# Two gated-convolution and feed-forward layers on one core: when plane loads are queued, how many dummies stand at the beginning, and in which order transposes run

## The chip, the core and the metric

The kernel runs on one core of a Trainium2 chip. The core has five engines with queues of their own: PE (matmuls; PEld is its weight load), DVE, ACT and POOL (vector, activation and general work) and SP, which here only issues DMAs. POOL issues DMAs too, between its small operations. The metric is the device time of one execution in microseconds (us).

## What is computed

Two layers, each a gated long convolution (A) and a feed-forward block (B), on 2048 tokens of 576 features, in bfloat16. The inner width of B is 4608. Cut to what matters:

```python
def A(q, k, v):
    k_shift = sum(k_pad[:, t:t + S, :] * shift_k[:, 3 - t] for t in range(4))
    kv = k_shift * v
    y = irfft(rfft(kv, 2 * S) * rfft(ssm_k, 2 * S))[:S] + kv * ssm_D
    return q * y

def B(x):
    return (gelu(x @ w_gate) * (x @ w_up)) @ w_down

x = x + A(layernorm(x), A_k, A_v);  x = x + B(layernorm(x))
x = x + A(layernorm(x), A_k, A_v);  x = x + B(layernorm(x))
```

## The kernel before

**Tiling.** The tokens are cut into four chunks of 512 (`CH`). One layer of one chunk is a unit; eight units run in five passes. A pass goes three times through a third of the inner width (12 tiles of 128, `FP`): first `gu`, the gate and up products (L1010: for each tile 18 matmuls of 64 rows and 512 columns, gate and up side by side in the two halves of the array, 1.94 us a tile), then `dn`, the product with `w_down` (L1603, 96 matmuls of 288 columns). All units read all weights again. `load_wgu` (L778) brings four tiles' weights in three DMAs of SP's queue (576, 512 and 64 KB) into one of three buffers, `load_wd` (L788) half a third of `w_down`.

**The convolution.** It is computed once for both layers, chunk by chunk (m = 0 to 3), as block products in the frequency domain. The filter's block transforms lie in DRAM as planes `Hd[b][t]`, those of kv as `Kd[b][t]`. `Conv.step(m)` puts the work of a chunk into lists: `L` (loads), `V` (DVE: kv, then products `prod` at L316 to L320 of a kv plane and a filter plane) and `Pq` (PE: forward transforms L301, inverse L343). For a product of an earlier chunk's kv, `load(kt, a)` issues two DMAs on POOL's queue: a kv plane into `kr` (L418, three buffers) and a filter plane into `hr` (L422, four buffers), 288 KB each; for a product of its own kv only the second. The products of chunk m read the transforms `kc` of that chunk as well, marked in `at` under `("kc", kt, s, h)` when their making is planned.

**What sets the order.** The whole program is written out in advance. `Pace` keeps a planned time for PE (`t.pe`), DVE and ACT. Between matmuls `fill` (L1069) calls `weights()` (issues what `when_due` has put down and that is due), `conv.run_loads()` (pops `L` while its first entry's ready time is reached; before that `flush` writes out what is due of `spills`, a list of POOL work: stores and the small operations `nm`, `ve` and `rstd` of the layer norms), and then DVE, ACT and PE work as far as the planned times allow. The order in which these calls come is the order on each engine's queue. On the chip only semaphores count: an instruction waits for its operands and buffers, and everything behind it on its queue waits with it. `hurry()` is true while the second chunk's convolution isn't finished.

**Layer norm.** For each 128 tokens: `x_c` (DVE L894) is made by the gate, `nm` (POOL L842) is the mean, `junk` (ACT L850) sums squares, `ve` and `rstd` (POOL L857, L858) follow, then `xn` (DVE L923) and its transposition `xnT` by two DMA transposes of SP's queue (L965), which the next unit's `gu` reads.

**The beginning.** Up to about 47 us the order comes from `Plan.order`, a list scheduler with durations and priorities. 20 dummy matmuls (L1141) run first; then come the taps (L1199, which spread the shift weights over the partitions) with two dummies (`spare`, L1192), the sum of the shifted products (L1228), transposes of the filter (L1257 for the first 512 positions, L1277 for the next), the forward transforms (L281, L275), the inverse (L1363), dummies in `busy` (L1382) and the transposes of the first `xn` (L1467, L1469). D = 576 is four times 128 and a rest of 64, so a transposition over D has blocks of 128 and of 64 rows; `turn_xn` has eight full blocks and, for b = 4, two halves of 64 columns.

Of the kernel before, what the change touches and what calls it, by code (L numbers as in the profile page):

```python
# [17 lines left out]
P = 128  # L18
# [8 lines left out]
NEVER = 1e9  # L27
# [10 lines left out]
LAG = 0.25  # L38
AHEAD = 2.0
SLOW, PRESS = 6.0, 22.0  # L40
HOLD, SOON, LEAD, FAR = 14.0, 30.0, 1.8, 3.6


class Pace:
# [88 lines left out]
class Conv:  # L133
# [9 lines left out]
    def __init__(self, tc, ctx, pace, A_k, A_v, A_shift_k, A_ssm_k, A_ssm_D, ident, cps, ypool):  # L143
        self.tc, self.nc, self.t = tc, tc.nc, pace
        self.k2, self.v2, self.hk = A_k[0], A_v[0], A_ssm_k
        self.S, self.D = self.k2.shape
        self.NB = self.S // BS
        self.KS = A_shift_k.shape[1]
        self.sk, self.sD = A_shift_k, A_ssm_D
        self.ident, self.cps, self.ypool = ident, cps, ypool  # L150
        D = self.D
        pool = lambda name, bufs: ctx.enter_context(tc.tile_pool(name=name, bufs=bufs))
        self.cst = pool("c_cst", 1)
        self.krp = pool("c_kr", 3)
        self.hrp = pool("c_hr", 4)
        self.kcp = pool("c_kc", N_KC)
        self.ybp = pool("c_yb", 4 * RT)
        self.prp = pool("c_pr", 3)
        self.acp = pool("c_ac", 3)
        self.eop = pool("c_eo", 2)  # L160
        self.kvp = pool("c_kv", 1)
        self.Hd = [[tc.dram_tile([P, 2 * D], BF16, name=f"Hd{b}_{t}") for t in range(RT)] for b in range(self.NB)]
        self.Kd = [[tc.dram_tile([P, 2 * D], BF16, name=f"Kd{b}_{t}") for t in range(RT)] for b in range(self.NB - 1)]
        self.hs = {b: tc.dram_tile([BS, D], BF16, name=f"hs{b}") for b in range(2, self.NB)}
        self.T = self.cst.tile([P, RT, 2, P], BF16, name="T")
        self.nT = self.cst.tile([P, 5, P], BF16, name="nT")
        self.V_ = self.cst.tile([P, 2, RT, P], BF16, name="V")
        self.nV = self.cst.tile([P, 3, P], BF16, name="nV")
        self.skc = self.cst.tile([P, self.KS, D], BF16, name="skc")
        self.y, self.yb, self.hh = {}, {}, {}  # L170
        self.kt_, self.vt_ = {}, {}
        self.y_at = {(0, j): 0.0 for j in range(RT)}
        self.z_at = {0: 0.0}
        self.kv_at, self.fwd_at, self.hf_at, self.hd_at = {}, {}, {}, {}
        self.ht = {}
        self.y_used = {}
        self.ps_free, self.cur, self.alt, self.alt_at = [0.0, 0.0], 0, None, None
        self.neo, self.eo_at = 0, deque([0.0] * 2)
        self.U = deque()
        self.kr_free, self.hr_free = [0.0] * 3, [0.0] * 4  # L180
        self.nkr = self.nhr = 0
        self.V, self.L, self.Pq = deque(), deque(), deque()
        self.left = 0
        self.spills = deque()
# [184 lines left out]
    def step(self, m, kv=None, loaded=False):  # L369

        nc, D, t = self.nc, self.D, self.t
        kc, kr, hr, z, nyb, prs = {}, {}, {}, {}, {}, {}
        KTS = (0, 2, 1, 3)
        at = {}
# [48 lines left out]
                at[("ld", kt, a)] = t.pe + 8.0  # L423
            return run
        for kt, a in pairs:
            self.L.append((lambda a=a: max(self.hr_free[self.nhr % 4], self.hd_at.get(m, NEVER) if a == 0 else 0.0,
                                           self.kr_free[self.nkr % 3] if a < m else 0.0),
                           load(kt, a)))

# [100 lines left out]
        w = {}  # L530
# [165 lines left out]
def ssm_geglu_kernel(ctx, tc, A_q, A_k, A_v, A_shift_k, A_ssm_k, A_ssm_D, B_x, B_w_gate, B_w_up,  # L696
# [4 lines left out]
    S, D = q2.shape  # L701
# [9 lines left out]
    NKC = D // HK  # L711
# [8 lines left out]
    t = Pace()  # L720
# [33 lines left out]
    def pr(name):  # L754
        while late and taken[0] - late[0][1] >= 2:
# [15 lines left out]
    conv = Conv(tc, ctx, t, A_k, A_v, A_shift_k, A_ssm_k, A_ssm_D, ident,  # L771
                lambda *form: bank(turn[3], "cps", *form), ypool)
# [274 lines left out]
    def weights():  # L1047

        while due:
            near = xn_made or (vq and isinstance(vq[0][0], tuple) and vq[0][0][0] == "xn")  # L1050
            if due[0][0] > t.pe + (HOLD if near else SOON):
                break
            _, _, load, n = due.pop(0)
            load(n)

    coming, due_at = [0], [0.0]

# [33 lines left out]
    with tc.manual_schedule():  # L1091
# [3 lines left out]
        ND = D // P + 1  # L1095
        plan = Plan(4)
        add = plan.add
        with ExitStack() as es:
# [38 lines left out]
            warm = tmp.tile([P, 1], F32, name="warm")  # L1137
            nc.scalar.activation(out=warm[:], in_=conv.pis[:], func=ACT.Sin)
            ps = bank(3, "ps")
            for _ in range(20):  # L1140
                nc.tensor.matmul(ps[:, 0, 0:P], lhsT=ones[:], rhs=ones[:], start=True, stop=True)  # L1141

            held = {}
# [44 lines left out]
            vneg = add("ACT", 0.9, vnegs, [vsin], prio=-20.0)  # L1188

            def spare(ps):  # L1190
                for _ in range(2):
                    nc.tensor.matmul(ps[:, 1, 3 * P:4 * P], lhsT=ones[:], rhs=ones[:], start=True, stop=True)  # L1192


# [15 lines left out]
            for i0 in range(0, RT, 2):  # L1210
                accs = {i0: [], i0 + 1: []}
                first = {}
                for j in range(conv.KS - 1, -1, -1):
# [9 lines left out]
                    for i in (i0, i0 + 1):  # L1223
# [7 lines left out]
                        a = later(lambda me: add("PE", 0.25, me(acc), [mults[-1]], bank=(j == conv.KS - 1), prio=20.0))  # L1231
# [16 lines left out]
            def turned_h0():  # L1248
                outs = []
                hT[0] = lambda i: hT0[:, i, :]  # L1250
                for g in range(RT // 2):
                    def fill_ps(task, g=g):
                        pt = psum(("h", g), task, (P, 2, 1024), BF16)
                        for i in range(2):
                            for db in range(ND):
                                w = min(P, D - db * P)
                                nc.tensor.transpose(pt[:, i, db * P:db * P + w], hn[0][0:w, db, 2 * g + i:BS:RT], ident[0:w, 0:w])  # L1257
                    a = later(lambda me: add("PE", 1.05, me(fill_ps), bank=True, ready=HN_AT, prio=30.0))
                    outs.append(add("ACT", 1.12, lambda g=g: nc.scalar.copy(out=hT0[:, 2 * g:2 * g + 2, :], in_=held.pop(("h", g))[:, :, 0:D]),
                                    [a], lat=0.1, frees=[a], prio=30.0))  # L1260
                return outs

            def turned_h1(dep):


                W = D - P
                beside = lambda j: held["y", j].bitcast(BF16)
                hT[1] = conv.ht[1] = lambda i: pairs1[i // 2][:, i % 2, :]
                for g, j in ((0, 3), (1, 1)):
                    def fill_ps(g=g, j=j):  # L1270
                        pairs1.append(conv.hrp.tile([P, 2, D], BF16, tag="hr", name="ht"))
                        for i in range(2):
                            for db in range(ND):
                                w = min(P, D - db * P)
                                out = beside(j)[:, i, 2 * HW + (db - 1) * P:2 * HW + (db - 1) * P + w] if db else \
                                    beside(0)[:, g, 2 * HW + i * P:2 * HW + (i + 1) * P]
                                nc.tensor.transpose(out, hn[1][0:w, db, 2 * g + i:BS:RT], ident[0:w, 0:w])  # L1277
                    a = add("PE", 1.0, fill_ps, dep + [opened[0], opened[j], facs[j]], prio=-30.0)
                    add("DVE", 0.2, lambda g=g: nc.vector.tensor_copy(
                        out=pairs1[g][:, :, 0:P], in_=beside(0)[:, g, 2 * HW:2 * HW + 2 * P].rearrange("p (i d) -> p i d", i=2)),  # L1280
                        [a], frees=[opened[0]], prio=-10.0)
                    add("ACT", 0.84, lambda g=g, j=j: nc.scalar.copy(
                        out=pairs1[g][:, :, P:D], in_=beside(j)[:, :, 2 * HW:2 * HW + W]), [a], lat=0.1, frees=[opened[j]], prio=-20.0 if g else -30.0)
# [25 lines left out]
            kc, A = {}, {}  # L1309
            K0 = {}  # L1310
            for m in KTS:
                K0[m] = []
                for s in range(2):
                    def fill_ps(task, m=m, s=s):
                        if s == 0:
# [3 lines left out]
                    a = later(lambda me: add("PE", 0.99, me(fill_ps), list(kv0.values()) + [tneg if m else tsin], bank=True,  # L1319
                                           prio=-4.0 * KTS.index(m)))  # L1320
# [85 lines left out]
            for j in (0, 2, 1, 3):  # L1406
# [52 lines left out]
                def turn_xn(task, j=j):  # L1459
                    if 0 not in xnT_of:  # L1460
                        xnT_of[0] = xtp.tile([P, NKC, CH], BF16, tag="xnT", name="xnT")
                    pt = psum(("xt", j), task, (P, 2, 1024), BF16)
                    for b in range(NKC):
                        c0 = b * P if b < 5 else HK + (b - 5) * P
                        if b == 4:
                            for r0, c0 in ((0, 4 * P), (HK, 0)):
                                nc.tensor.transpose(pt[r0:r0 + HK, 0, 4 * P:5 * P], held["xn", j][:, c0:c0 + HK], ident[:])  # L1467
                            continue
                        nc.tensor.transpose(pt[:, b // 8, (b % 8) * P:(b % 8 + 1) * P], held["xn", j][:, c0:c0 + P], ident[:])  # L1469
# [49 lines left out]
        hurry = lambda: (1, RT - 1) not in conv.y_at  # L1519
# [4 lines left out]
        for at, (wb, ph, ui, first, final) in enumerate(visits):  # L1524
# [33 lines left out]
            for fi in range(FP):  # L1558
                n, gi = divmod(wb * FP + fi, FG)
                w = wgu[n]  # L1560
# [141 lines left out]
```

## Time and profile before

| | |
|---|---|
| median of 3 runs (lowest, highest) | 926.32 us (924.35, 926.99) |
| the profiled execution | 929.08 us |
| its span, from the first to the last instruction | 927.3 us |
| PE busy | 917.8 us |
| gu (L1010), busy; dn (L1603), busy | 563.6 us; 294.1 us |
| granted clock of PE, mean | 0.996 |
| DMA moved | 129.69 MB |

The profile's page gives busy times by engine, the chain of work that ended last, and groups of instructions. Other views of the same trace are the timeline (start, length, engine, line, operation, tiles, count, and in brackets the idle time before it and what ended it), the list of waits (in total, times, longest) and windows (busy time of each engine in a stretch). A matmul's length includes its way through the array; the distance of two starts is what it costs in a row. The clock column counts only what the profiler recorded.

### The profile page before, as it was taken

The page shows a single profiled execution, that of the slowest core. Times are in us where ns is not written, and L with a number is a line of the kernel's source. Part 1 is how long each engine was busy: PE and PEld are TensorE (multiplying, and loading weights), DVE is VectorE, ACT ScalarE, POOL GpSimd, SP SyncE. Part 2 cuts the span into 40 slices and gives each one's busy share as a digit, 9 for nine tenths or more (in the row PEclk, how much of TensorE's full clock was granted, in tenths as well). Part 3 has the DMA queues.
Part 4 walks back from the last instruction along what each step waited for, and adds up shares of the span by engine and source line. Part 5 has one row for each costly group of instructions (what it writes and reads, how often), then busy time and mean ns, then how long its engine had stood idle before and what let it go on. Part 6 is the DMA issues. An engine that isn't in the chain of part 4 may idle for free.

```text
span 927.3 us, 19211 instructions
## 1 busy us (share of the span) xinstructions
PE 917.8 (99%) x8085; PEld 526.5 (57%) x8085; DVE 558.8 (60%) x1106; ACT 364.7 (39%) x675; POOL 141.2 (15%) x314
## 2 busy tenths in 40 slices
PE   9999999999999999989999999999999999999998
PEld 6746556465565564636646646546556556556555
DVE  7885887883889886548988943553332334433332
ACT  6774436635425366344253332451221224321211
POOL 4413102320114012410121101220000002100000
PEclk9999999999999999989999999999999999999999
DMA  9999997369518602982953720692820731777640
GB/s 231 274 243 204 265 269 165 91 177 205 179 54 201 165 1 40 271 171 72 244 172 100 136 78 27 125 158 52 153 78 2 144 87 14 132 175 180 125 106 27
DMA packets 125307, 129.69 MB, mean 140 GB/s; under 512 B 39714, under 2 KB 117411, under 8 KB 125220
## 3 DMA queue, kind: packets, MB, share of 16 engines
q1 hardware_dynamic: 116018, 92.92, 47.9%
q0 software_dynamic: 9056, 34.95, 11.7%
q8 instruction: 63, 1.03, 0.5%
q10 hardware_dynamic: 146, 0.59, 0.2%
q14 instruction: 24, 0.20, 0.1%
HBM read 108.09 MB, written 11.80 MB: 129 GB/s over the span
## 4 chain that ended last, share of the span: by engine, by line
PE 94%; DMA 4%; issue 1%; ACT 0%; DVE 0%; POOL 0%; SPq 0%; ACTq 0%; POOLq 0%; DVEq 0%
PE gu L1010 58%; PE dn L1603 30%; DMA wgu<-in_B_w_up_dram 2%; DMA Hd<-hh 2%; PE ps L281 1%; PE cps L343 1%; PE cps L301 1%; PE ps L1228 1%; PE ps L1363 1%; PE ps L1010 0%; PE ps L1257 0%; DMA sk<-in_A_shift_k_dram 0%; PE cps L290 0%; PE ps L275 0%; PE ps L1277 0%
## 5 line engine op out<-in xcount | busy, mean ns | idle before, releaser
L1010 PE MATMUL gu<-xnT,wgu 64*128 64x512 bf16 x5148 | 563.6, 377 | 4.4 <-DMA wgu<-in_B_w_up_dram 4.0
L1010 PEld LDWEIGHTS <-wgu 64*128 64x128 bf16 x5220 | 252.2, 94 | 312.1 <-issue 9.9
L1603 PE MATMUL dn<-wd,hT 128*128 128x288 bf16 x2304 | 294.1, 286 | 0.0
L1603 PEld LDWEIGHTS <-hT 128*128 128x128 bf16 x2304 | 223.6, 98 | 65.0 <-issue 7.2
L1584 ACT ACTIVATE ga<-gu 128x512 f32<-128x512 f32 x175 | 104.5, 597 | 331.2 <-PE gu L1010 328.1
L1585 DVE TENSOR_TENSOR hT<-ga,gu 128x512 bf16<-128x512 f32 x175 | 120.2, 687 | 183.7 <-ACT ga L1584 183.6
L1574 ACT ACTIVATE ga<-gu 128x512 bf16<-128x512 f32 x111 | 66.4, 598 | 156.2 <-PE gu L1010 148.5
L1576 DVE TENSOR_TENSOR hT<-ga 128x512 bf16<-128x512 bf16 x112 | 47.0, 422 | 61.5 <-ACT ga L1575 61.2
L1575 ACT CAST ga<-gu 128x512 bf16<-128x512 f32 x111 | 64.4, 581 | 0.0
L842 POOL TENSOR_SCALAR means<-s 128x1 f32<-128x1 f32 x28 | 9.5, 341 | 245.0 <-DVE x_c L1639 206.9
L1647 DVE TENSOR_TENSOR x_c<-x_c,dn 128x576 f32<-128x576 f32 x32 | 24.1, 752 | 27.4 <-PE dn L1603 27.2
L1645 DVE SCALAR_TENSOR_TENSOR x_c<-dn,means,x_c 128x576 f32<-128x576 f32 x28 | 22.8, 816 | 26.2 <-PE dn L1603 26.2
L858 POOL TENSOR_TENSOR rstd<-ve,neghalf_t 128x1 f32<-128x1 f32 x56 | 34.9, 623 | 4.7
L320 DVE TENSOR_TENSOR prod<-prod 128x576 bf16<-128x576 bf16 x72 | 33.0, 458 | 2.5
L303 ACT ACTIVATE eo<-cps 128x576 f32<-128x576 f32 x32 | 20.5, 654 | 20.9 <-DVE ab L308 9.2
L1626 DVE TENSOR_TENSOR xn<-x_c,dn 128x576 bf16<-128x576 f32 x15 | 11.3, 754 | 27.9 <-PE dn L1603 27.9
L418 POOL DMA_DIRECT2D kr<-Kd x24 | 13.2, 552 | 85.0 <-DVE prod L319 84.6
L604 DVE TENSOR_TENSOR kc<-ab,cd 128x288 bf16<-128x288 f32 x64 | 25.4, 453 | 0.0
L422 POOL DMA_DIRECT2D hr<-Hd x36 | 19.6, 547 | 36.9 <-DVE prod L319 36.6
L842 POOL TENSOR_SCALAR nm<-s 128x1 f32<-128x1 f32 x28 | 8.5, 305 | 94.3 <-DVE x_c L894 94.3
L884 ACT ACTIVATE yh<-y,rstd 128x576 f32<-128x576 bf16 x28 | 21.4, 769 | 2.6 <-POOL rstd L858 2.3
L850 ACT ACTIVATE junk<-x_c,nm 128x576 bf16<-128x576 f32 x28 | 21.5, 767 | 2.0 <-POOL nm L842 1.9
(180 smaller groups left out, 611.6 us busy)
## 6 DMA issues: line engine op xcount, KB each, us to landing
wgu<-in_B_w_gate_dram SPq DMA_DIRECT2D x45, 576.0 KB, 6.3
wd<-in_B_w_down_dram SPq DMA_DIRECT2D x30, 864.0 KB, 7.1
wgu<-in_B_w_up_dram SPq DMA_DIRECT2D x45, 512.0 KB, 8.3
hr<-Hd POOLq DMA_DIRECT2D x36, 288.0 KB, 6.4
kr<-Kd POOLq DMA_DIRECT2D x24, 288.0 KB, 4.3
Kd<-kc POOLq DMA_DIRECT2D x12, 288.0 KB, 5.3
k<-in_A_k_dram POOLq DMA_DIRECT2D x3, 1008.0 KB, 11.2
wgu<-in_B_w_up_dram SPq DMA_DIRECT2D x45, 64.0 KB, 8.5
```

Of the source, the lines that this page charges most:

```text
L320: nc.vector.tensor_tensor(out=dst[:, cols], in0=pr[:, 0, cols], in1=pr[:, 1, cols], op=ALU.subtract if part == 0 else ALU.add)
L604: nc.vector.tensor_tensor(out=into[k][:, plane, cols], in0=a, in1=b, op=op)
L858: nc.gpsimd.tensor_tensor(out=v["rstd"][:], in0=ve[:], in1=neghalf_t[:, 0:1], op=ALU.pow)
L1010: nc.tensor.matmul(cols(pair[:, s, :]), lhsT=w[r0:r0 + HK, k, gi * P:(gi + 1) * P], rhs=cols(xnT[r0:r0 + HK, blk_of[k], :]), start=(k == 0 ...
L1574: nc.scalar.activation(out=ga[:, 0, :], in_=pair[:, 0, :], func=ACT.Gelu_apprx_tanh)
L1575: nc.scalar.copy(out=ga[:, 1, :], in_=pair[:, 1, :])
L1576: nc.vector.tensor_tensor(out=hT[:, fi, :], in0=ga[:, 0, :], in1=ga[:, 1, :], op=ALU.mult)
L1584: nc.scalar.activation(out=ga[:], in_=pair[:, 0, :], func=ACT.Gelu_apprx_tanh)
L1585: nc.vector.tensor_tensor(out=hT[:, fi, :], in0=ga[:], in1=pair[:, 1, :], op=ALU.mult)
L1603: nc.tensor.matmul(acc[:, h, 0:HW], lhsT=hT[:, fi, j * P:(j + 1) * P], rhs=wd[2 * wb + fi // WT][:, fi % WT, h * HW:(h + 1) * HW], start=( ...
L1645: nc.vector.scalar_tensor_tensor(out=xh, in0=acc[:, :, 0:HW], scalar=m_[:, 0:1], in1=xh, op0=op, op1=ALU.add)
L1647: nc.vector.tensor_tensor(out=xh, in0=xh, in1=acc[:, :, 0:HW], op=ALU.add)
```

## The change

Planned loads of planes get one more condition. `weights()` now sets `conv.quiet` to ten planned microseconds after each weight load that it issues, unless `hurry()`; a plane load of `step` isn't popped before `quiet` unless the transform `("kc", 0, 0, 0)` of its chunk is planned already. In the program that results, DVE, ACT and SP have the same instructions in the same order as before. On POOL one place differs: seven plane loads (three `kr`, four `hr`) of chunk 3 stood ahead of three `nm`, one `ve` and one `rstd`, and now stand behind these five.

```
before: out_dram, kr, hr, kr, hr, kr, hr, hr, nm, nm, nm, ve, rstd, ve, rstd, nm, ve, rstd
after:  out_dram, nm, nm, nm, ve, rstd, kr, hr, kr, hr, kr, hr, hr, ve, rstd, nm, ve, rstd
```

The dummies at the beginning are 24, not 20, and those of `spare` 5, not 2. In L1257 and L1277 the loop over the blocks of D goes outside, so that the four blocks of two tiles come in a row: eight transposes of 128 rows and then two of 64, where before it was four, one, four, one. In `turn_xn` block 4 comes last: eight full ones and then the two halves, where before the halves stood between four and four.

```diff
-HOLD, SOON, LEAD, FAR = 14.0, 30.0, 1.8, 3.6
+HOLD, SOON, QUIET, LEAD, FAR = 14.0, 30.0, 10.0, 1.8, 3.6
...
+        self.quiet = 0.0
...
         for kt, a in pairs:
-            self.L.append((lambda a=a: max(self.hr_free[self.nhr % 4], self.hd_at.get(m, NEVER) if a == 0 else 0.0,
+            self.L.append((lambda a=a: max(0.0 if ("kc", 0, 0, 0) in at else self.quiet, self.hr_free[self.nhr % 4], self.hd_at.get(m, NEVER) if a == 0 else 0.0,
                                            self.kr_free[self.nkr % 3] if a < m else 0.0),
                            load(kt, a)))
...
             _, _, load, n = due.pop(0)
             load(n)
+            if not hurry():
+                conv.quiet = t.pe + QUIET
...
-            for _ in range(20):
+            for _ in range(24):
                 nc.tensor.matmul(ps[:, 0, 0:P], lhsT=ones[:], rhs=ones[:], start=True, stop=True)
...
             def spare(ps):
-                for _ in range(2):
+                for _ in range(5):
                     nc.tensor.matmul(ps[:, 1, 3 * P:4 * P], lhsT=ones[:], rhs=ones[:], start=True, stop=True)
...
-                        for i in range(2):
-                            for db in range(ND):
-                                w = min(P, D - db * P)
+                        for db in range(ND):
+                            w = min(P, D - db * P)
+                            for i in range(2):
                                 nc.tensor.transpose(pt[:, i, db * P:db * P + w], hn[0][0:w, db, 2 * g + i:BS:RT], ident[0:w, 0:w])
...
-                    for b in range(NKC):
+                    for b in sorted(range(NKC), key=lambda b: b == 4):
```

The loop at L1272 to L1277 is turned in the same way as that of L1257.

More of the change, by code (lines that the diff above doesn't have):

```diff
@@ L1271, in fill_ps @@
                         pairs1.append(conv.hrp.tile([P, 2, D], BF16, tag="hr", name="ht"))
-                        for i in range(2):
-                            for db in range(ND):
-                                w = min(P, D - db * P)
+                        for db in range(ND):
+                            w = min(P, D - db * P)
+                            for i in range(2):
                                 out = beside(j)[:, i, 2 * HW + (db - 1) * P:2 * HW + (db - 1) * P + w] if db else \
```

## The prediction

> **What bounds the kernel now.** I read the page first, then PE's waits, then the two places that these name.
>
> ```profile
> PE 917.8 (99%) x8085; PEld 526.5 (57%) x8085; DVE 558.8 (60%) x1106; ACT 364.7 (39%) x675; POOL 141.2 (15%) x314
> PE 94%; DMA 4%; issue 1%; ACT 0%; DVE 0%; POOL 0%; SPq 0%; ACTq 0%; POOLq 0%; DVEq 0%
> ...
> PE gu L1010 <- DMA wgu<-in_B_w_up_dram: 4.0, 1, 4.0
> PE gu L1010 <- DMA wgu<-in_B_w_gate_dram: 0.3, 1, 0.3
> ```
>
> PE is busy for 99% of the span, so time can come only from three things: PE work that goes, idle of PE, and PE work done at a lower rate. The list of waits has one idle of size: 4.0 us, once, for a weight load. In time, it stands here: PE's timeline, then windows (length, busy time of PE, PEld, DVE, ACT and POOL, granted clock, DMA share, GB/s).
>
> ```profile
> 383.41 15.71 PE L1010 MATMUL gu<-xnT,wgu 64*128 64x512 bf16 x144
> 399.44 0.39 PE L1010 MATMUL gu<-xnT,wgu 64*128 64x512 bf16 x1 [0.32 <-DMA wgu<-in_B_w_gate_dram]
> 403.88 10.26 PE L1010 MATMUL gu<-xnT,wgu 64*128 64x512 bf16 x71 [4.05 <-DMA wgu<-in_B_w_up_dram]
> ...
> 399.00:401.80 2.80, 0.51 (x3) 0.09 (x1) 2.22 (x7) 0.60 (x1) 0.95 (x3) 1.00 1.16 167
> 401.80:408.60 6.80, 4.72 (x24) 1.73 (x26) 0.00 (x0) 0.61 (x2) 0.00 (x0) 0.50 1.27 202
> 408.60:412.00 3.40, 3.40 (x34) 1.53 (x32) 1.79 (x4) 1.82 (x4) 0.97 (x2) 1.00 0.62 61
> ```
>
> The stall costs more than its idle. 71 matmuls take 10.26 us, where the row before has 144 in 15.71 (0.109 each, 7.75 for 71): the granted clock was 0.50 from 401.8 to 408.6, and PE worked 403.88 to 408.6 at half rate, a loss of 4.72 / 2 = 2.36. The place as a whole costs 0.32 + 4.05 + 2.36 = 6.7 us. What delayed the load is read from SP's timeline, the chain (one line, start and length) and POOL's timeline:
>
> ```profile
> 380.28 0.91 SPq L783 DMA_DIRECT2D wgu<-in_B_w_gate_dram  x1
> 381.24 3.51 SPq L784 DMA_DIRECT2D wgu<-in_B_w_up_dram  x1
> ...
> 381.24 22.59 DMA wgu<-in_B_w_up_dram
> ...
> 385.10 0.55 POOL L418 DMA_DIRECT2D kr<-Kd  x1
> ...
> 394.83 0.19 POOL L857 TENSOR_SCALAR ve<-ss 128x1 f32<-128x1 f32 x1 [1.03 <-ACT junk L850]
> 395.11 0.57 POOL L858 TENSOR_TENSOR rstd<-ve,neghalf_t 128x1 f32<-128x1 f32 x1
> 396.72 0.19 POOL L857 TENSOR_SCALAR ve<-ss 128x1 f32<-128x1 f32 x1 [1.04 <-ACT junk L850]
> ```
>
> The weight load of 1152 KB (576 + 512 + 64) is issued at 380.28 and lands 22.59 us after its second part, where the page's median is 6.3 to 8.5. Between 385.10 and 389.2 POOL issues seven plane loads (three kr, four hr, 288 KB each, 2016 KB); they land 8.6 to 13.2 us after issue, so by 401.9, beside the weights. The second place is the beginning, in PE's timeline:
>
> ```profile
> 1.08 2.31 PE L1141 MATMUL ps<-ones 128*128 128x128 bf16 x20 [1.08 <-DVE ones L1113]
> 3.61 2.20 PE L1199 MATMUL ps<-sk,ones 97*128 97x288 bf16 x8 [0.22 <-DMA sk<-in_A_shift_k_dram]
> 5.63 0.39 PE L1192 MATMUL ps<-ones 128*128 128x128 bf16 x2
> 6.09 1.11 PE L1228 MATMUL ps<-kvt,below 128*128 128x288 bf16 x4
> 7.00 2.96 PE L1257 MATMUL ps<-ident,hn 128*128 128x128 bf16 x20
> 12.71 0.61 PE L1184 MATMUL ps<-ident,T 128*128 128x128 bf16 x8
> ```
>
> Matmuls of 128 columns start every 0.107 us up to here (20 in 2.1) and every 0.056 from 12.71: PE runs at half rate for its first 11.6 us, though the clock column shows 1.00 there (the records begin later). Holes are small: 0.22 at 3.39, 0.06 at 6.03, and in L1257 each change between 128-row and 64-row transposes.
>
> **The change, part by part.** *Plane loads behind weights.* Every queue keeps its order and its waits but POOL's (and PE's, below). There three nm, one ve and one rstd pass ahead of the seven loads. These five are ready no earlier than now (nm at 389.66 to 393.60 after DVE, ve at 394.83 after ACT), so the loads are issued from 395.11 + 0.57 = 395.7 on, 10.6 us later, to about 399.5 (seven of 0.55). Their bytes are gone from the stretch in which the weights come. The windows of 5 us from 386 on show 262 to 308 GB/s; 2.06 MB at 300 is 6.9 us, so the last part lands at about 403.8 - 6.9 = 396.9. A second estimate: two such loads issued at 598.8 and 600.9, without planes, land 7.8 and 11.5 us after issue of their last parts, 5.7 us apart; the load before ours lands at 391.05 now, plus 5.7 is 396.8. PE needs it at 399.1: covered by 2.2 us. Gain 6.7, all there is. The lower bound is 2.4: the two estimates are off by 4 us, 2.0 of the 4.4 us of idle and the half rate stay. A loss here is excluded, since no byte is added ahead of the load.
>
> What is moved and what it now meets: the second ve and rstd, 396.72 to 397.54 now, stand behind the loads and end at about 399.5 + 0.9 = 400.4. Their reader is DVE's second xn (L923), which starts at 400.50 after a product of hT: free, by 0.1 us. Uncovered, each us would push the hT products behind it, of which PE stands one bank (1.94 us) off. The third rstd comes at 401.4, its xn about 6.7 us earlier than 409.23: free by 1. The planes land some 10 us later, by about 411; the first product that reads them (L316) starts at 435.39, 428.7 with the gain: free by 17. The transposes of xnT (L965, first at 399.27) meet the planes where they met weights and planes; their longest now is 8.6 us, the last issue would be at 409.4, the landing by 418, the next gu at 427.9 - 6.7 = 421.2: free by 3.
>
> *Transposes.* L1257 in the cold stretch: a visit to the 64-row form takes 0.244 + 0.170 + 0.089 for three starts, against 0.107 + 0.107 + 0.053 without a change: 0.24 each, four visits become two, 0.47 off PE. L1228 behind it has its operand at 9.10 and starts at 9.89, so that it can follow. If the half rate still ends at 12.7, work that slides in front of it runs cold, and half of the 0.47 remains: 0.25. L1277 (four visits of 0.385 for 0.167): 0.44 off PE at 38.5, but the DVE copy behind it can start only when the xn before it ends (39.43 against 39.55): 0.13. The xn transposes L1467 lose their last change before gu: 0.15 to 0.17 less 0.15 that L1010 then pays: 0. Sum 0.4; bounds 0.1 and 0.9.
>
> *Dummies.* Four more at 0.107 are 0.43 us in the hole before L1199, whose operand comes at 3.48 and which starts at 3.61: the last one starts at 3.50, cost 0 (0.1 at most). Three more behind the first tap: 0.32 us from 5.82, L1228 slides from 6.09 to 6.14: cost 0.05. The ACT copy of that tap waits for them too, 0.3 us, and its product on DVE comes at about 7.1: covered. What they can bring is an earlier full rate. No row shows such a thing with these holes filled, so bounds: 0, and for full rate from 6 us on 2.6. The latter because ACT then binds: its sine ends at 7.75, two copies of 1.12 and the table load of 1.28 follow, so the V copy comes at 11.5, not 13.36, and with 0.74 us of ACT idle at 17.28 that is 1.9 + 0.7. For one step of 3.4 us earlier it is about 1.5. The restart after the stall is the nearest row: full rate came back 4.7 us after matmuls went on without a hole. By it a stretch without holes from 1.08 to 7.5 would be enough. But 97 of 128 rows in L1199 and the transposes may count for less. I take 1.0.
>
> [...]
>
> **Sum.** Against the profiled execution's own 929.08 us (span 927.3 and 1.8 around it): 6.7 + 0.4 + 1.0 = 8.1, 921.0. The median of the runs shown, 926.32, is 2.8 below that execution. Part of this may be a smaller stall, since its half-rate share hangs on when the clock falls: between 0.32 + 4.05 = 4.4 without it and 6.7. I take 6.0 for timed runs: 926.3 - 6.0 - 0.4 - 1.0 = 918.9.
>
> **Rivals.** *A: the weights still come late* (the loads before them, wd behind them and four out stores crowd the queue as well; SP needs 3.51 us to issue one part, before any plane load stands there). For: the load is slow from 380.3 on, planes from 385.1. Against: the 2.2 us of cover. Price: 1 to 2 us of idle and the half rate are left, gain 2.4 to 3.3: 923.5. *B: only the beginning moves or nothing does*, the stall being smaller in runs that aren't profiled. For: the 2.8 us between them. Against: bytes and order are the same. Gain 0 to 1.5: 925.5. *C, slower: the planes now crowd xnT.* All seven start with the transposes at 395.7 to 399.5. If the last xnT comes later than 421.2, PE idles at the next gu and loses clock as at 401.8; with half rate (2.4) it needs 5 us of idle to eat up 7.4, a landing at 426, 17 us after issue. Against: 8.6 is the longest now with more bytes in flight. 928. *D, within the forecast: no earlier full rate:* 919.9; with it 917.5 to 918.4.
>
> **Chances.** Forecast 0.80 (D half of it), A 0.10, B 0.06, C 0.04. Low end: 6.7 + 0.9 + 2.6 = 10.2 below 926.3 is 916.1, less some of the runs' spread (924.35 to 926.99): 915.5. High end 923.5, where A stands. A measurement of this kernel tells 0.3% (2.8 us, 923.5) from no change. Faster: 0.80 + half of A + a little of B, 0.86; same: 0.09; slower: C and strays, 0.05.
>
> **What would show it.** PE's list of waits without L1010 <- wgu; no 0.50 clock near 400; kr and hr issued at 395.7; xn's second L923 still at about 400.5; L1277 shorter by 0.4; the step from 0.107 to 0.056 us per dummy or transpose before 9.3 (or still near 12.7: D). A wait of gu near 421 would be C, one near 399 A.

## The result and the profile after

The changed kernel takes 918.76 us (median of 9 runs, 918.59 to 922.95), the kernel before 925.8 (9 runs, 921.59 to 927.67): ratio 0.9936, 95% interval 0.9917 to 0.9954, so 4.3 to 7.7 us less. The profiled executions differ by more: 929.08 before and 918.68 after, 10.4 us, with spans of 927.3 and 916.9. All but one of the nine runs after lie within 1 us of each other; the one at 922.95 has a granted clock of 0.998 where the others have 0.999 or 1.0.

The page of the changed kernel, busy times and the chain that ended last by engine:

```profile
PE 911.7 (99%) x8092; PEld 524.9 (57%) x8092; DVE 558.5 (61%) x1106; ACT 364.2 (40%) x675; POOL 142.6 (16%) x314
...
PE 99%; POOL 0%; ACT 0%; DVE 0%; issue 0%; ACTq 0%
```

PE's list of waits, whole:

```profile
PE ps L1144 <- DVE ones L1116: 1.1, 1, 1.1
PE ps L1472 <- DVE xn L1458: 0.5, 2, 0.3
```

(Line numbers are one higher from the constructor of the planner on and three higher in the beginning.) The wait for wgu has left the list, and DMA has left the chain. PE's busy time fell by 6.1 us though it runs 7 matmuls more: what fell is in the main the part at half rate, at the beginning and behind the stall. PE's timeline of the pass that held the stall:

```profile
380.30 23.48 PE L1011 MATMUL gu<-xnT,wgu 64*128 64x512 bf16 x216
```

POOL's timeline there:

```profile
391.99 0.57 POOL L859 TENSOR_TENSOR rstd<-ve,neghalf_t 128x1 f32<-128x1 f32 x1
392.52 0.63 POOL L419 DMA_DIRECT2D kr<-Kd  x1
...
396.98 0.56 POOL L859 TENSOR_TENSOR rstd<-ve,neghalf_t 128x1 f32<-128x1 f32 x1
```

And the issue of the last part of the weights, with its time to landing:

```profile
L786 SPq DMA_DIRECT2D wgu<-in_B_w_up_dram x1: 1052/1052/1052, 380.7 to 380.7; - x1
...
DMA to landing us min/median/max: 12.9/12.9/12.9
```

The pass is now 216 matmuls without a break in 23.48 us. Plane loads begin when the first rstd is done; the weights land at 380.7 + 12.9 = 393.6, where PE, 15.7 us into its pass (its matmuls before the stall took 15.71), needs them at 396.0.

The beginning in PE's timeline:

```profile
1.08 2.74 PE L1144 MATMUL ps<-ones 128*128 128x128 bf16 x24 [1.08 <-DVE ones L1116]
3.88 2.20 PE L1202 MATMUL ps<-sk,ones 97*128 97x288 bf16 x8
5.90 0.46 PE L1195 MATMUL ps<-ones 128*128 128x128 bf16 x5
6.36 0.65 PE L1231 MATMUL ps<-kvt,below 128*128 128x288 bf16 x4
6.84 1.62 PE L1260 MATMUL ps<-ident,hn 128*128 128x128 bf16 x20
9.88 0.61 PE L1187 MATMUL ps<-ident,T 128*128 128x128 bf16 x8
```

The half rate ends before 6 us: five dummies of 128 columns now fit into 0.46, four matmuls of 288 columns into 0.65 (1.11 before). The trace's clock record begins at 5.03 us, with full rate; before, at 12.67. From the starts of the same instructions in both timelines the 10.4 us can be laid out:

| start of | before | after | earlier by |
|---|---|---|---|
| the first matmul with weights | 42.88 | 40.11 | 2.77 |
| the second gu pass | 87.67 | 84.55 | 3.12 |
| the gu pass with the stall | 383.41 | 380.30 | 3.11 |
| the next gu pass | 427.90 | 417.54 | 10.36 |

So 2.8 us come from the beginning, 0.35 from the stretch up to the second pass (in the kernel before PE waits there for ACT's `eo`, 0.2 us at 83 us), and 7.25 from the stalled pass.

### The profile page after: what moved, and what is told of

Same layout as the page of the kernel before. It is cut to its first block, busy times and chain, and to the rows that moved or that the text cites. A ratio compares the mean times of both kernels' runs of the same rounds, so it can differ in the third digit from the quotient of the medians.

```text
span 916.9 us, 19225 instructions
## 1 busy us (share of the span) xinstructions
PE 911.7 (99%) x8092; PEld 524.9 (57%) x8092; DVE 558.5 (61%) x1106; ACT 364.2 (40%) x675; POOL 142.6 (16%) x314
## 4 chain that ended last, share of the span: by engine, by line
PE 99%; POOL 0%; ACT 0%; DVE 0%; issue 0%; ACTq 0%
PE gu L1011 61%; PE dn L1606 31%; PE ps L282 1%; PE cps L291 1%; PE cps L344 1%; PE cps L302 1%; PE ps L1231 0%; PE ps L1011 0%; PE ps L1366 0%; POOL rstd L1451 0%; PE ps L1144 0%; PE ps L1202 0%; PE ps L276 0%; PE cps L1027 0%; ACT yh L1413 0%; PE ps L1260 0%
## 5 line engine op out<-in xcount | busy, mean ns | idle before, releaser
L419 POOL DMA_DIRECT2D kr<-Kd x24 | 13.3, 554 | 85.8 <-DVE prod L320 84.1
```

## Experiments

Times are medians, ratios are to the kernel before as it ran beside each set of experiments. Its medians there were 925.8 (with the changed kernel), 926.13 (e1 to e4), 926.38 (e5 to e8) and 927.65 (e9 to e12; 8 runs), so a difference of about 1 us between rows of different sets isn't shown by the times alone. "First gu" is the start of the first matmul with weights, "full rate" the begin of the clock's record, both from the profiled execution; "pass" is the time from the start of the gu pass near 380 us to the start of the next one. A window, in the expectations and below, is a stretch of 3.41 us: the half clock lasted that long in e2's profile (0.50 from 400.0 to 403.4) and twice that, 6.83 us, in the kernel before (401.79 to 408.62).

| label | us (runs) | ratio, interval | first gu | full rate | pass |
|---|---|---|---|---|---|
| before | 926.13 (35) | | 42.88 | 12.67 | 44.49 |
| after | 918.76 (9) | 0.9936, 0.9917 to 0.9954 | 40.11 | 5.03 | 37.24 |
| e1_loads | 921.79 (12) | 0.9951, 0.9931 to 0.9970 | 43.23 | 13.58 | 37.24 |
| e2_begin | 923.17 (12) | 0.9967, 0.9946 to 0.9987 | 40.04 | 4.07 | 41.83 |
| e3_dummies | 923.12 (12) | 0.9964, 0.9947 to 0.9980 | 40.47 | 5.12 | 41.92 |
| e4_transposes | 926.08 (12) | 1.0008, 0.9986 to 1.0030 | 39.62 | 5.72 | 44.14 |
| e5_24 | 925.13 (10) | 0.9977, 0.9955 to 0.9999 | 40.46 | 3.99 | 41.80 |
| e6_spare5 | 924.62 (10) | 0.9981, 0.9959 to 1.0004 | 40.38 | 6.57 | 44.06 |
| e7_two_early | 918.82 (4) | 0.9912, 0.9877 to 0.9946 | 40.04 | 5.12 | 37.24 |
| e8_four_early | 919.54 (7) | 0.9927, 0.9904 to 0.9949 | 40.03 | 5.19 | 37.78 |
| e9_no_dummies | 919.88 (5) | 0.9927, 0.9903 to 0.9952 | 41.28 | 9.93 | 37.24 |
| e10_20_5 | 920.36 (4) | 0.9923, 0.9899 to 0.9946 | 39.61 | 4.55 | 37.24 |
| e11_24_2 | 919.38 (4) | 0.9919, 0.9895 to 0.9942 | 40.03 | 4.25 | 37.24 |
| e12_no_busy | 918.88 (1) | | 40.28 | 6.77 | 37.24 |

### The plane loads alone, and the beginning alone

`e1_loads` is the changed kernel with this undone, and with the loops over transposes in the old order:

```diff
-            for _ in range(24):
+            for _ in range(20):
...
-                for _ in range(5):
+                for _ in range(2):
```

> Only the order of POOL's queue is changed; dummies and transposes are as before. Theory (planes delay the weights, the stall costs 4.4 to 6.7 us, of the timed gain of 7.0 it makes the larger part): gu no longer waits for wgu, the granted clock has no 0.50 stretch near 400 us, ratio to before 0.993 to 0.9955 (4 to 6.5 us). Rival (the timed gain is mainly the beginning's, the stall of the profiled execution was an unusually bad one): ratio 0.997 to 1.0, the rest comes with the dummies. Both: the clock's record begins where the phase of its windows puts it, near 9 to 16 us.

The stalled pass takes 37.24 us, as in the changed kernel, and PE's list of waits has no wgu:

```profile
PE ps L1144 <- DVE ones L1116: 1.1, 1, 1.1
PE ps L1472 <- DVE ht L1282: 0.2, 1, 0.2
```

The ratio is 0.9951, that is 4.3 us by the medians (2.8 to 6.4 by the interval): the theory's side, at its lower end. The runs spread from 918.61 to 925.15, with granted clocks of 0.999 or 1.0, so without a fall of the clock; the fastest two stand level with the changed kernel. What is left to spread them, as far as is known, is the beginning, by 3 us as the profiles have it; the slowest (925.15) isn't explained by that.

`e2_begin` keeps the dummies and the transposes and takes the condition on the loads out again:

```diff
-            self.L.append((lambda a=a: max(0.0 if ("kc", 0, 0, 0) in at else self.quiet, self.hr_free[self.nhr % 4], self.hd_at.get(m, NEVER) if a == 0 else 0.0,
+            self.L.append((lambda a=a: max(self.hr_free[self.nhr % 4], self.hd_at.get(m, NEVER) if a == 0 else 0.0,
```

> Dummies and transposes as in the changed kernel, plane loads where they were before. Theory: the stall of some 4 us stays, at a place about 3 us earlier, with half clock after it; gu at the beginning starts near 40 us as in the changed kernel (42.9 before); ratio 0.997 to 0.9985 (1.4 to 2.8 us). Rival (the beginning carries the gain): ratio 0.993 to 0.995.

PE's waits:

```profile
PE gu L1011 <- DMA wgu<-in_B_w_up_dram: 2.8, 1, 2.8
PE cps L291 <- ACT eo L294: 1.4, 1, 1.4
```

Windows of the stalled pass (length, busy time of PE, PEld, DVE, ACT, POOL, granted clock, DMA share, GB/s):

```profile
396.60:400.00 3.40, 1.13 (x11) 0.29 (x5) 3.01 (x8) 0.96 (x3) 0.96 (x3) 1.00 1.06 284
400.00:403.40 3.40, 2.89 (x14) 1.02 (x16) 0.00 (x0) 0.00 (x0) 0.00 (x0) 0.50 1.47 228
```

The stall is there again, with 3.4 us of half clock where the kernel before had 6.8, so that the pass costs 4.6 us too much and not 7.25. The beginning alone brings 3.0 us by the medians (0.9967), a bit over the theory's range and short of the rival's. Loads 4.3 and beginning 3.0 make 7.3; both together measure 7.0. In this execution 1.4 us of the gain are lost again at 81.6, where PE waits for ACT's `eo`, and it in turn for a store of hh planes that lands at 80.2 (77.0 in the changed kernel, issued within 0.1 us of the same time). e3 and e5 show the same wait (1.4 and 0.9), e4, e6 and the changed kernel none above 0.1. Why the store lands late in some executions stays open.

### Dummies and transposes apart

`e3_dummies` has 24 and 5 dummies and nothing else of the change, `e4_transposes` only the turned loops.

> Only the dummies: 24 for 20 and 5 for 2; transposes in the old order, planes early. Theory: full rate of PE comes at the first window's edge after 1.08 + 3.4 = 4.5 us, so between 4.5 and 7.9, and the first gu starts at 40.3 to 41.0 us (42.9 before, 40.1 with all of the change). Rival (the hole in the first 6 us does not matter, transposes with their changes of form are what keeps the clock down): full rate still between 9.9 and 16 us, first gu at 42.5 to 44. Stall stays. Ratio by the theory 0.9975 to 0.999.

> Only the transposes are turned, 20 and 2 dummies, planes early. Theory: PE's rate changes no earlier than in the kernel before (9 to 16 us, by the phase of the windows), the transposes L1257 and L1277 take 0.4 us less each, gu starts 0.2 to 0.5 us earlier than it would at the same clock; stall stays; ratio 0.9990 to 1.0, not told from 1. Rival (the changes of form are what keeps the clock down): full rate at 9.3 us or before, first gu at about 41.3.

e3 gives 0.9964, all that the beginning brings, a bit more than forecast, with full rate at 5.1 as forecast. e4 gives 1.0008: the transposes alone bring nothing that can be told. But its profiled execution has full rate at 5.72 with 20 and 2 dummies, where the rival wanted it (9.3 or before), and the earliest gu of that set. That doesn't speak for the rival: the first transposition starts at 6.42, so their order can't have raised the clock at 5.72. Its other runs (921.48 to 932.31) are as those of the kernel before. So early full rate is possible without the dummies and only not reliable; one profiled execution can't stand for the kernel here. e4's PE timeline shows also what four dummies at the front cost:

```profile
3.45 2.20 PE L1202 MATMUL ps<-sk,ones 97*128 97x288 bf16 x8
...
6.42 1.55 PE L1260 MATMUL ps<-ident,hn 128*128 128x128 bf16 x20
```

The taps start at 3.45; with 24 dummies at 3.88 in every profile. Where the clock rises in time anyway, that is 0.43 us lost: first gu at 39.6 in e4 and e10, at 40.0 to 40.1 with 24 and the loops turned (after, e2, e7, e8, e11).

What the turned loops are worth once the rate is full is seen in pairs of profiles in which it is full before the first transposition. The row of e4 above takes 1.55 us, as it does in e2; in e3, with the old order, it takes 2.04:

```profile
6.84 2.04 PE L1260 MATMUL ps<-ident,hn 128*128 128x128 bf16 x20
```

The first gu is 0.43 us earlier with the turned loops: 40.04 in e2 against 40.47 in e3, and 40.03 in e11 against 40.46 in e5. That is too little for the timed runs to tell.

`e5_24` and `e6_spare5` take one kind of dummy each.

> Only the first dummies: 24 for 20, two behind the first tap, transposes and planes as before. Closes the hole of 0.22 us at 3.4 us and leaves that at 6.0. Theory (a window of 3.4 us without a hole is what opens the clock): the stretch without a hole is 1.1 to 5.9, so full rate begins between 4.5 and 5.9 us if a window's edge falls there (it does for 4 of 10 phases), else later than 9. Rival (any window more than some 90% busy opens it, so the 0.22 us were what was missing): full rate between 4.5 and 7.9 in every execution.

> Only the dummies behind the first tap: 5 for 2; 20 at the front, transposes and planes as before. Leaves the hole at 3.4 us and closes that at 6.0. Theory: the stretch without a hole is 3.6 to 7.5, so a window of 3.4 us fits for 1 or 2 of 10 phases only; full rate mostly not before 9 us. Rival (what counts is one window's share, and transposes count for less): the same, but with a hole of 0.22 in 3.4 tolerated full rate between 4.5 and 7.9.

Each brings about half (0.9977 and 0.9981, neither well told from 1). Full rate came at 3.99 in e5 and at 6.57 in e6. Both go against the theory as written: at 3.99 the window of 3.41 us had begun at 0.57, half a microsecond before the first matmul, so a window without a hole isn't needed; and e6's window lay across the change from dummies to taps at 3.4. By these runs a share decides, then, and it can't be the share of time in which PE looks busy, for in e1 the window that ends at 10.17 is busy throughout (transposes, with changes of form) and did not raise the clock:

```profile
6.85 2.96 PE L1260 MATMUL ps<-ident,hn 128*128 128x128 bf16 x20
9.74 1.62 PE L1231 MATMUL ps<-kvt,below 128*128 128x288 bf16 x6
```

### What the clock counts

For each profile I cut the time before full rate into windows of 3.41 us, counted back from the begin of the clock's record, and summed over the matmuls columns / rate x rows used / 128, over 3.41 us. The length of a window is that of the stretches at half clock, 3.41 us in e2, e3 and e5 and twice that in the kernel before, e4 and e6; the rate at half clock is 1.2 columns per ns (128 in 0.107 us); at full clock I took twice that, since the granted clock is 1.00 against 0.50 (128 columns take 0.056 us there). The numbers are worked out from start times and shapes in the traces, transposes included:

```
window that raised the clock: after 0.83, e2 0.79, e3 0.83, e4 0.75, e5 0.77, e6 0.76, e7 0.82,
                              e8 0.82, e10 0.84, e11 0.83, e12 0.76, e9 0.83, before 0.93, e1 1.00
window just before it or earlier, that did not:
                              before 0.40 0.71 0.70, e1 0.62 0.74 0.69, e6 0.61, e9 0.60 0.70, e12 0.67
```

One limit near 0.75 parts all of them, though narrowly (0.743 in e1 against 0.747 in e4); it is an estimate from these windows. The limit was found from e1 to e8; the windows of e9 to e12, run afterwards, agree with it. Without the weight by rows it fails: e1's window up to 6.75 has 0.88 and didn't raise the clock, e5's has 0.78 and did. So a weight of 97/128, about three quarters, fits for the taps, as the prediction had it for possible; other weights near it aren't excluded.

`e9_no_dummies`, `e10_20_5` and `e11_24_2` are the changed kernel with the old number of dummies in both places or in one.

> The changed kernel with the old numbers of dummies (20 and 2); planes late, transposes turned. Theory (the clock opens at the first edge of a free-running window of 3.41 us in which PE's streams, weighted by the rows used, fill some 75%; the dummies make this so for every phase): times fall into two kinds, 918.2 to 918.8 where the edge falls well and 920 to 925 where it does not; median 1 to 3 us above the changed kernel's 918.8. Rival (once the stall is gone and transposes are turned, the dummies bring nothing): median 918.2 to 918.8, all runs within 1 us.

> The changed kernel with 20 dummies at the front and 5 behind the first tap. Theory (window weighted by rows, 75%): the windows that lie on the hole at 3.4 us are filled up by the five behind, as in the run with these alone (0.76 at an edge of 6.57 us); most runs within 1 us of 918.6, a few above 920. Rival: as the kernel with both old numbers.

> The changed kernel with 24 dummies at the front and 2 behind the first tap. Theory: windows with edges from about 5.5 to 7 us stay below 75%, since the taps use 97 rows of 128 and the hole at 6 us is open; some 3 to 4 of 10 runs 1.5 us or more above 918.6. Rival (the hole at 3.4 us was what mattered): all runs within 1 us of 918.6.

e9: 919.88, all five runs from 919.51 up, 1.1 us above the changed kernel's median. But the two ran in different sets, and by the ratios to the kernel before (0.9927 and 0.9936) e9 isn't slower, so that the timed runs don't show what the dummies are worth when the stall is gone; in the profiles the first gu is 1.17 us later without them (41.28 against 40.11). The two kinds of times did not show in five runs. PE's timeline of its profile:

```profile
6.84 2.48 PE L1260 MATMUL ps<-ident,hn 128*128 128x128 bf16 x20
9.26 1.22 PE L1231 MATMUL ps<-kvt,below 128*128 128x288 bf16 x6
10.31 0.90 PE L1231 MATMUL ps<-kvt,ident 128*128 128x288 bf16 x6
```

Full rate comes at 9.93, between the second row (1.22 for six) and the third (0.90), about one window earlier than in e1, which differs in the transposes' order alone. The window that raised it, 6.51 to 9.93, holds mostly transposes: 0.83 with them, 0.30 without; e1's from 6.75 to 10.17, with twice the changes of form, has 0.69. So transposes do count, and with fewer changes of form they fill enough of a window; that is what turning them can bring where the windows before them fail.

e11 has two runs at 918.6 and two at 920.2 and 920.8, as the theory has it, though four runs are few. e10 has one at 918.20, the fastest of this study, and three from 920.1 up; the theory wanted most near 918.6. By that the five behind the first tap don't fill the window as surely as I had worked out; only the fastest of the four was profiled, so that a late clock in the other three is inferred. Among e7 and e9 to e11 no version is told from the changed kernel: the medians lie 0.1 to 1.6 us above its own, the ratios (0.9912 to 0.9927) below its 0.9936, within the intervals.

What the profiles say is this: with 24 dummies at the front full rate began by 6.8 us in all eight, with 20 between 4.55 and 13.58 in six.

`e12_no_busy` takes away the 16 dummies between the transposes of the filter and those of xn.

> The changed kernel without the 16 dummies between the transposes L1280 and L1472 (0.7 us of matmuls that compute nothing used). Between 33.8 and 40.1 us PE then runs transposes alone, with waits. Theory (transposes count for the clock as their streams fill it, 0.5 to 0.6 of a window, and the clock closes only below about 0.4): it stays open, the time is that of the changed kernel within 0.5 us. [...]

PE's timeline:

```profile
34.01 1.75 PE L1280 MATMUL ps<-ident,hn 128*128 128x128 bf16 x20
36.82 0.62 PE L1471 MATMUL ps<-ident,xn 128*128 128x128 bf16 x8 [1.05 <-DVE xn L1457]
```

Windows of the same stretch:

```profile
34.10:37.50 3.40, 2.30 (x31) 1.74 (x29) 3.30 (x13) 3.40 (x10) 2.73 (x6) 1.00 0.98 337
37.50:40.90 3.40, 3.06 (x44) 2.24 (x44) 2.71 (x6) 3.40 (x5) 1.29 (x3) 1.00 1.00 209
```

The clock stays at 1.00 through two windows of transposes and waits, and the time, of one run, is 918.88. In the measure above the two windows have 0.40 and 0.65; without their transposes they would have 0.00 and 0.18, as little as the windows around the stalls (0.15 to 0.25), after which the clock fell each time. The theory holds.

### How many planes it takes

`e7_two_early` and `e8_four_early` let the first pair, or the first two pairs, of the seven loads through without the condition (`a < 1`, in e8 `a < 2`):

```diff
-            self.L.append((lambda a=a: max(0.0 if ("kc", 0, 0, 0) in at else self.quiet, self.hr_free[self.nhr % 4], self.hd_at.get(m, NEVER) if a == 0 else 0.0,
+            self.L.append((lambda a=a: max(0.0 if a < 1 or ("kc", 0, 0, 0) in at else self.quiet, self.hr_free[self.nhr % 4], self.hd_at.get(m, NEVER) if a == 0 else 0.0,
```

> The changed kernel, but two of the seven plane loads (576 KB) are queued where they were before, five behind the norms. Theory (bytes in front of the weights delay them at about 300 GB/s, 1 us for each load): the last weights land 2 us later than in the changed kernel (393.6 there, needed at about 396), so still in time: no wait, no 0.50 clock, time as the changed kernel (918.5 to 919.5). Rival (the planes' queue as such takes a share from the weights' queue, whatever its length): a wait of 1 us or more.

> The changed kernel, but four of the seven plane loads (1152 KB) are queued where they were before. Theory: the last weights land 4 us later than in the changed kernel, at about 397.5, 1 to 2 us after PE needs them: a wait of 1 to 2 us; the clock falls or not, as the window's phase has it, so 1 to 4 us more than the changed kernel. Rival (only the planes that land last, those behind the weights, matter, or the queue's share): no wait, or the whole 4 us.

The issue of the weights' last part in e7, with its time to landing:

```profile
L786 SPq DMA_DIRECT2D wgu<-in_B_w_up_dram x1: 1058/1058/1058, 380.6 to 380.6; - x1
...
DMA to landing us min/median/max: 14.8/14.8/14.8
```

The same in e8:

```profile
L786 SPq DMA_DIRECT2D wgu<-in_B_w_up_dram x1: 1001/1001/1001, 380.4 to 380.4; - x1
...
DMA to landing us min/median/max: 16.2/16.2/16.2
```

And in e8's list of PE's waits:

```profile
PE gu L1011 <- DMA wgu<-in_B_w_up_dram: 0.2, 1, 0.2
```

Counted from the start of the pass the weights land after 13.3 us with no plane early, 14.9 with two, 16.4 with four, 19.0 with all seven (e2) and 20.8 in the kernel before: 0.8 to 1.1 us for each load of 288 KB. The kernel before owes some of its 20.8 to SP, which issued the last part 1.4 us after the start of the pass, against 0.1 to 0.6 in the others; counted from that issue the landing takes 12.9 us with no plane early, then 14.8, 16.2, 18.5 (e2) and 19.4, 0.8 to 1.0 for each load. PE needs the weights after 15.7. So the price goes by the number of bytes moved beside them, and two loads on the other queue don't make a wait (e7). Four loads cost a wait of 0.15 us and no clock, 0.7 us by the medians against e7 of the same set, less than the 1 to 4 expected; two cost nothing that can be told.

## Why the prediction was right, and where its terms were off

*The stall* was the right place and the right cause. Without planes the weights were to land at 396.9 in the old times, which is 393.8 after 3.1 us of earlier start; they land at 393.6. (The second estimate has a slip: the 7.8 and 11.5 us belong to the second of the three parts, and these land 5.8 apart, at 607.26 and 613.06. It changes 0.1 us.) *Its size* was off in two ways. I counted the idle of the list, 0.32 + 4.05, and the half rate, 6.7 in all; start to start the pass lost 7.25. Most of the difference, 0.38, lies in front of the restart: from 383.41 to 403.88 the pass took 20.47 us for 145 matmuls, which make 15.72 at the later passes' 23.42 for 216, and the two waits make only 4.37 of the 4.75 more. And for timed runs I took 6.0; e1 measures 4.3 to 4.5. The reason given, that the part at half rate hangs on when the clock falls, agrees with the runs: of 65 runs of the kernel before beside these experiments, 46 have a granted clock of 0.998 (one window at half), 11 of 0.996 (two), 7 of 1.0 (none) and 1 of 0.994, with medians 926.25, 929.05 and 925.17 for the first three. The profiled execution had two.

*The beginning* I took at 0.4 for the transposes + 1.0 for the dummies; it measures 3.0 (interval 1.2 to 5.0), 2.8 in the profile, inside the bound of 3.5. The term that was too small is the dummies': alone, in e3, they bring 3.3 (1.9 to 4.9) in timed runs and 2.4 in the profile (first gu at 40.47 against 42.88). The value I took was a cut between no effect and one step of the clock (3.4 us, as long as e2's half clock lasted). The kernel before needed more steps in both profiles with its beginning, with full rate at 12.67 and 13.58.

*The sum for timed runs* met by luck: by the medians the stall was 1.6 too much and the beginning 1.6 too little, and the two cancelled: 7.4 was forecast and 7.0 came. The intervals of e1 (2.8 to 6.4) and e2 (1.2 to 5.0) would just hold both terms as forecast; that of e3 doesn't hold 1.0 for the dummies.

*The sum against the profiled execution* was 8.1 and 10.4 came. The 2.3 missing are 1.4 at the beginning, 0.55 in the stalled pass and 0.35 in the stretch between, which had no term. The 2.8 us between that execution and the median are no price of profiling, since the changed kernel's profiled execution lies at its median; 929.08 is where the runs of the kernel before with two windows at half clock lie (median 929.05). So rival B had it right that the stall is smaller in most runs, and not that nothing of it is left there: 4.3 by e1.

*The transposes* brought what was forecast, as far as profiles show it: 0.43 us at the first gu in two pairs (0.4 was forecast), L1277 to L1280 0.3 less with a wait of 0.2 in it. In timed runs it can't be told (e4: 1.0008, interval 0.9986 to 1.0030). *The dummies* in front were costed at 0, since the last was to start at 3.50; twenty-four end at 3.82, past the operand at 3.48, and the taps start 0.27 us later than in the profile before, 0.43 later than in the other profiles with 20.

*What was moved* stayed covered: the second rstd was to come at 400.4 in old times, 397.3 in new ones, and comes at 397.5, its xn at 397.6. The transposes of xnT all land by 409.0 where the next gu starts at 417.5, so what rival C feared didn't come; A's wait near 399 isn't in the list either.

## What to carry to other kernels

A late load on the bounding engine can cost more than its wait: in the kernel before two waits of 4.4 us in all cost 7.25, with a granted clock of 0.50 for 6.8 us. So look at the granted clock beside the wait and move bytes that nobody needs yet behind it. Where a kernel's runs spread by some us, one profiled execution is one draw; ask which of its costs hang on a phase before using it as the base. Dummies at the start can buy an earlier clock, here by 6.8 us in every profile with 24, and are worth only what the gap takes: the four more in front cost up to 0.43 us where the clock would have risen in time.

## What the runs showed of the hardware

- In the clock's records of both kernels the changes of PE's granted clock lie whole multiples of 3.413 us apart: 389.12, 6.83 and 518.83 before, 911.36 after, that is 114, 2, 152 and 267 times. It rose after a window in which columns x rows used fill 0.75 or more (14 windows from 0.75 to 1.0 raised it, 10 from 0.40 to 0.74 did not); the limit is an estimate worked out from these same windows.
- It fell after windows far below that: six of 0.15 to 0.25, around the stalls, were each followed by half clock, and so was one of 0.31 at the very end of e11 (912.2 to 915.6); one of 0.40 (e12, 34.1 to 37.5) was not. After the fall, windows of 0.40, 0.61 and 0.64 did not raise it again.
- Half clock lasted one window in e2's profile (2.8 us of wait), two in the kernel before (4.05) and in e4 (3.8). Whether it came at all varied from run to run of one kernel: four of e2's twelve runs have a granted clock of 1.0 (921.15 to 922.10), eight 0.998 (922.95 to 926.50).
- In these windows transposes on PE counted as other matmuls did (e9: 0.83 with them, 0.30 without; e12: 0.40 and 0.65 with them, 0.00 and 0.18 without); what lowered the share is the change between 128 and 64 rows, 0.24 us a visit at half rate (20 transposes in 2.96 us with four visits in e1, in 2.48 with two in e9).
